# Gated GELU feed-forward: the last Strassen product of six unit pairs in the second pass is divided once more

## The chip, the cores and the metric

The kernel runs on one core of one Trainium2 chip. The metric is the device time of one execution in microseconds. Three runs of the kernel before took 538.74, 539.11 and 539.6 us; the median is 539.11 us. One execution was also recorded by the profiler, and all rows below are from it.

## The reference

```python
def reference(x, w_gate, w_up, w_down):
    g = einsum("bsd,df->bsf", x, w_gate)      # S = 2048 tokens, d = 1024, f = 3584
    u = einsum("bsd,df->bsf", x, w_up)
    h = gelu(g) * u                           # tanh form of gelu
    return einsum("bsf,fd->bsd", h, w_down)   # 2048 x 1024
```

Inputs, weights and the result are bf16. The arithmetic is three products of 2048 x 1024 x 3584.

## The kernel before

The 2048 tokens are taken in two passes of 1024 (two halves of N = 512). A pass first makes `h` for all 3584 features and keeps it in SBUF (`hT`), then multiplies it with `w_down` (`down`, line 464). Both steps use Strassen's scheme in Winograd's form: a product of 2 x 2 blocks is made of seven block products instead of eight, with sums of blocks ahead of and behind them.

Gate/up goes by units: unit `u` has 256 columns of `w_gate` and 256 of `w_up`, fourteen units in a pass. The blocks of a unit are 128 features by 512 of the 1024 input rows on the weights' side (`a11`, `a21`, `a12`, `a22` in `sums_s`, line 150) and 512 input rows by 512 tokens on the other (`sums_t`, line 135). On the weights' side the sums `s1` to `s4` are made for every unit by POOL: eight operations of 128 x 512, since each exists for gate and for up. The sums of the tokens, `t1` to `t4`, are made once per pass by DVE. Sums are f32r, so products of sums are f32 matmuls; the two products of raw blocks are bf16. A product is four matmuls of 512 columns per output bank, one for each 128 input rows (`product`, line 186).

The PE order in a unit (`unit`, line 208) is: the product s2·t2 (P2), which accumulates on the bank of the raw product of unit and `xT`; s1·t1 (P5); s3·t3 (P7); s4·tb (P3); and sa·t4 (P4), which is the block A22 times T4. Each is eight matmuls, four for gate and four for up. The raw products of two units (32 bf16 matmuls, `raw_products`) are issued together, ahead of P4 of each odd unit (`ahead_of_p4`, line 682). So the work repeats by pairs of units, from one raw block to the next.

Results leave PSUM in this manner: ACT copies a bank to SBUF (`snap`), DVE adds another bank to the copy (`add`, line 199), ACT applies gelu, and DVE multiplies gate and up into `hT` (`times`). The eight PSUM banks are four pairs with changing roles `E`, `K`, `C`, `F` (lines 635 and 692).

Small tiles share one ring of 52 slots (`kpool`): a new tile takes the slot of the tile made 52 tiles before, and its first writer waits until all readers of that one are through. Weights of a unit lie in a ring of three buffers (`wpool`); SP issues the load of unit u+2 during unit u (`aside(0)`), and it waits for the buffer in the same way. The instructions of SP, DVE, POOL and PE, and in the unit loop of ACT too, run in the order in which the code names them; no scheduler moves them. In the first pass the unit loop also makes the sums of `w_down` (`keep_part`, `keep_whole`, `fetch_wd`, `store_made`), which go to DRAM and come back in both passes.

The last product of the second pass's `down` is itself divided once more already (`inner_product`, line 417): seven products with 256 columns, four of which go to halves of banks (`z1`, `z6`, `z7`, `z5`).

Of the kernel before, what the change touches and what calls it, by code (L numbers as in the profile page):

```python
# [10 lines left out]
def kernel(  # L11
# [5 lines left out]
    w_down: bass.AP,  # L17
    out: bass.AP,
):

    nc = tc.nc
# [19 lines left out]
    N = 512  # L55
    NS = N // P
    NPASS = S // (2 * N)
    NU = NFB // 2
    NWARM = 7
    H, Q, R2 = NJ // 2, N // 2, range(2)  # L60
    SLOTS = 52
    LAG = 3
# [27 lines left out]
    def dve(out, a, b, op):  # L90
        nc.vector.tensor_tensor(out=out, in0=a, in1=b, op=op)  # L91
# [4 lines left out]
    def new(eng, a, b, op, name, shape=None, dtype=None):  # L96
        t = slot(shape or [P, N], dtype or f32r, name)
        eng(t, a, b, op)
        return t

    def cast(src, name, shape=None):
        t = slot(shape or [P, N], f32r, name)
        nc.scalar.copy(out=t, in_=src)  # L103
        return t

    def snap(ps, name):
        t = slot([P, N], f32, name)
        nc.scalar.copy(out=t, in_=ps)  # L108
        return t
# [4 lines left out]
        )  # L114

    def load_w(u, queue=nc.sync):
        f0 = u * 2 * P
        w = wpool.tile([P, 2, NKB, 2 * P], bf16, name="w")  # L120
# [29 lines left out]
    def sums_s(w, eng):  # L150
        GU = range(2)
        sh = [P, KH, P]
        a11, a21 = [[w[:, i, :KH, h : h + P] for i in GU] for h in (0, P)]
        a12, a22 = [[w[:, i, KH:, h : h + P] for i in GU] for h in (0, P)]
        return Sums(
            how={
                "s1": lambda q, GU=GU: [new(eng, a21[i], a22[i], ADD, "s1", sh) for i in GU],
                "s2": lambda q: [new(eng, q["s1"][i], a11[i], SUB, "s2", sh) for i in GU],
                "s3": lambda q: [new(eng, a11[i], a21[i], SUB, "s3", sh) for i in GU],
                "s4": lambda q: [new(eng, a12[i], q["s2"][i], SUB, "s4", sh) for i in GU],  # L160
                "sa": lambda q: [cast(a22[i], "sa", sh) for i in GU],
            }
        )

    def pool_behind(tile):
        nc.gpsimd.tensor_copy(out=seen, in_=tile[:, :1].bitcast(f32))
# [3 lines left out]
        t.make("t1", "t2", "t3", "tb", "t4")  # L170
        return t

    def make_s(w, eng):
        s = sums_s(w, eng)
        s.make("s1", "s2", "s3", "sa", "s4")
        return s

    def gelu(src):
        g = slot([P, N], f32, "g")
        nc.scalar.activation(g, src, ACT.Gelu_apprx_tanh)  # L180
        return g

    def times(fb, c, g, u):
        dve(hT[:, fb // NJ, fb % NJ, c, :], g, u, MUL)

    def product(ps, lhs, rhs, start):
        for k in range(KH):
            matmul(ps, lhs[:, k, :], rhs[k], start and k == 0, k == KH - 1)

    def raw_products(e, c, xT, w):  # L190
        for i in range(2):
            product(e[i], w[:, i, :KH, :P], [xT[0][:, k, :] for k in range(KH)], True)
        p1 = [snap(e[i], "p1") for i in range(2)]
        for i in range(2):
            b21 = [xT[0][:, KH + k, :] for k in range(KH)]
            product(c[i], w[:, i, KH:, :P], b21, True)
        return p1

    def add(ps, other):
# [4 lines left out]
    def finish_raw(u, c, p1):  # L204
        g, up = add(c, p1)
        times(2 * u, 0, gelu(g), up)

    def unit(u, banks, s, t, late, after_p5, aside, keep, ahead_of_p4, behind_p4):
        GU = range(2)
        e, c, d = banks  # L210
        aside(-2)
        g, up = late() if late else (None, None)
        aside(-1)
        for i in GU:
            product(e[i], s["s2"][i], t["t2"], False)
        aside(0)
        keep(0, c[0])
        u2 = [snap(e[i], "u2") for i in GU]
        if late:
            g = gelu(g)  # L220
        c11 = g, up
        keep(1, c[0])
        keep(2, c[1])
        c = d
        for i in GU:
            product(c[i], s["s1"][i], t["t1"], True)
        p5 = [snap(c[i], "p5") for i in GU]
        after_p5()
        for i in GU:
            product(e[i], s["s3"][i], t["t3"], False)  # L230
        g, up = new(dve, e[0], p5[0], ADD, "sum", dtype=f32), banks[1][not late]
        dve(up, e[1], p5[1], ADD)
        if late:
            times(2 * u, 0, *c11)
        for i in GU:
            product(c[i], s["s4"][i], t["tb"], False)
        times(2 * u + 1, 1, gelu(g), up)
        aside(1)
        g, up = add(c, u2)
        times(2 * u, 1, gelu(g), up)  # L240
        ahead_of_p4()
        for i in GU:
            product(e[i], s["sa"][i], t["t4"], False)
        behind_p4()
        times(2 * u + 1, 0, gelu(e[0]), e[1])

    td = dpool.tile([P, NJ, 3, N], f32, name="td")  # L250
    wraw, made = {}, {}
# [29 lines left out]

    def store_made(j):
        nc.sync.dma_start(out=td[:, j], in_=made[j][:, :3].bitcast(f32))

    q12, s12, q73, q4, raw = {}, {}, {}, {}, {}
# [43 lines left out]
    def fetch12(n):  # L331
# [1 line left out]
        rl = slot([P, 2, N], bf16, "raw")  # L333
        nc.sync.dma_start(out=rl, in_=wdn[:, kh, j : j + 2, :N])
        raw[1, n] = rl

    def inner_sums(late):
# [184 lines left out]
                put21(i)  # L524

    warm = nc.const_aps.tensor(1.0, [P, N], bf16)
    ident = xpool.tile([P, P], bf16, name="ident")  # L530
    make_identity(nc, ident)
# [98 lines left out]
    def making(u):  # L630
        if u < 2 or u >= NU:
            return []
        return list(range(u - 2, NJ if u == NU - 1 else u - 1))

    E, K, C, F = odd, cc, dd, even

    def loaded(u):
        if u not in ws:
            ws[u] = load_w(u)
        return ws[u]  # L640

    def raw_of(u, e):
        p1 = raw_products(e, K, xT, loaded(u))
        return lambda: finish_raw(u, K, p1)

    for ip in range(NPASS):
        with tc.manual_schedule(engines={ENG.Activation}):
            if ip == 0:
                ws = {1: w, 2: ahead}
                late = lambda: add(cc, nxt["p1"])  # L650
            else:
                raw_of(0, F)()
                raw_of(1, C)()
            for u in range(1 if ip == 0 else 0, NU):
                js = making(u) if ip == 0 else []
                first = (ip, u) == (0, 1)

                def prepare():
                    if first:
                        pool_behind(t["t4"][-1])  # L660
                    if u + 1 < NU:
                        nxt["s"] = make_s(loaded(u + 1), pool)
                    if len(js) == 1:
                        store_made(js[0])
                    for j in js[1:]:
                        keep_whole(j)
                    if ip == 0:
                        fetch_wd(making(u + 1))

                def keep(part, ps):  # L670
                    if js:
                        keep_part(js[0], part, ps)

                def aside(part):
                    if first and part < 0:
                        rest_of_0(part + 2)
                    if part == 0 and u + 2 < NU:
                        loaded(u + 2)
                    if part == 0 and "t4" not in t:
                        t.make("t4")  # L680

                def ahead_of_p4():
                    if u % 2 and u + 1 < NU:
                        raw_of(u + 1, F)()
                        nxt["c11"] = raw_of(u + 2, C)

                def behind_p4():
                    if "c11" in nxt:
                        nxt.pop("c11")()

                if u % 2 and not first:
                    E, K, C = C, E, K
                banks = (E, K, C) if u % 2 else (F, K, E)
                unit(
                    u, banks, s, t, late if first else None, prepare, aside, keep,
                    ahead_of_p4, behind_p4,
                )
                s = nxt.pop("s", None)

        last = ip == NPASS - 1  # L700
        got, nxt = {}, {}

        def more(step):
            if last:
                return
            if step in (-1, 0, 2):
                store_made({-1: NJ - 3, 0: NJ - 2, 2: NJ - 1}[step])
            if step == 0:
                xT[:] = new_x()
            if step >= 24 and step % 2 == 0 and step // 2 - 12 < len(moves):  # L710
                c, ko = moves[step // 2 - 12]
                transposing(xT, c, ko, (2 * (ip + 1) + c) * N)
            if step == 50:
                ws.clear()
                ws.update({n: load_w(n) for n in range(2)})
            if step == 58:
                got["s"] = make_s(ws[0], dve)
            if step == 62:
                got["t"] = make_t(xT)

        down(ip, F + K, C + E, last, more)
        E, K, C, F = K, E, F, C
        if not last:
            t, s = got["t"], got["s"]

# [28 lines left out]
```

## Time and profile before

| | |
|---|---|
| median of three runs | 539.11 us (538.74 to 539.6) |
| profiled execution | 539.29 us |
| its span in the profile | 537.5 us (1.79 us lie around it) |
| granted TensorE clock | 0.999 |
| PE busy | 532.7 us, 99% of the span |
| DVE, POOL, ACT busy | 356.3 (66%), 259.3 (48%), 258.1 (48%) |
| second-pass gate/up, 270 to 446 us | PE busy 176.00 of 176.00 us, POOL 119.38, ACT 97.03, DVE 94.79 |

The first 7 us are loads and transposes, 7 to 270 us are the first pass, 270 to 446 us gate/up of the second, and the rest its down product.

How to read it: PE and PEld are the matmuls and the weight loads of TensorE, DVE is VectorE, ACT ScalarE, POOL GpSimd, SP the engine that issues DMAs. Matmuls are pipelined and their ends are modelled, so that the mean duration of a record (390 to 401 ns for 512 f32 columns) is longer than the distance from one start to the next; costs are read from the starts. L112 is the line of the matmul helper, L91 that of DVE's operations, L94 that of POOL's, L108 ACT's copy out of PSUM, L180 gelu. A number in brackets at a row's end is idle time ahead of it, and what ended it. A row "x16" holds sixteen instructions one after another.

### The profile page before, as it was taken

The numbers are of one execution on the slowest core, as the hardware profiler recorded it, in microseconds if no ns is written. First come the engines' busy times: TensorE is split into PE (matmuls) and PEld (weight loads), VectorE is DVE, ScalarE is ACT, GpSimd is POOL, SyncE is SP. The second block draws the span as 40 slices with busy tenths as digits, with TensorE's granted clock in tenths as the row PEclk, the third lists the DMA queues.
The fourth block names the chain that finished last, engine by engine and source line by source line (L and its number), as shares of the span: only waits on it lengthen the run. The fifth ranks groups of instructions, "written<-read, shape, count | busy, mean of one in ns | idle before, by whom it ended". The sixth has DMA issues, their size and how long they took to land.

```text
span 537.5 us, 7573 instructions
## 1 busy us (share of the span) xinstructions
PE 532.7 (99%) x2451; PEld 382.4 (71%) x2451; DVE 356.3 (66%) x536; ACT 258.1 (48%) x457; POOL 259.3 (48%) x243
## 2 busy tenths in 40 slices
PE   8999999999999999999999999999999999999997
PEld 4568686867777746888868677776868685478887
DVE  2986766767676894595855464555554639979844
ACT  2556675666666410265355555555555551113340
POOL 1179966677773500000087767676766600000194
PEclk9999999999999999999999999999999999999999
DMA  9675666759482999999873233242520049573752
GB/s 245 156 186 168 186 177 176 218 136 262 131 234 71 383 357 298 308 197 275 264 187 88 78 80 81 77 119 50 145 57 23 2 130 390 204 236 88 243 169 70
DMA packets 108199, 93.30 MB, mean 174 GB/s; under 512 B 17280, under 2 KB 93056, under 8 KB 108160
## 3 DMA queue, kind: packets, MB, share of 16 engines
q1 hardware_dynamic: 108160, 92.82, 59.6%
q8 instruction: 20, 0.33, 0.3%
q14 instruction: 19, 0.16, 0.1%
HBM read 74.45 MB, written 15.20 MB: 167 GB/s over the span
## 4 chain that ended last, share of the span: by engine, by line
PE 98%; DMA 1%; SPq 0%; DVE 0%; issue 0%
PE bank L112 98%; DMA xn<-in_x_dram 1%; SPq L538 0%; DVE st L91 0%; PE bank L545 0%
## 5 line engine op out<-in xcount | busy, mean ns | idle before, releaser
L94 POOL TENSOR_TENSOR s<-w 128x512 fp32r<-128x512 bf16 x102 | 119.0, 1188 | 163.0 <-PE bank L112 113.5
L112 PE MATMUL bank<-t,s 128*128 128x512 f32 x648 | 151.7, 390 | 0.0
L112 PEld LDWEIGHTS bank<-t,s 128*128 128x128 f32 x648 | 121.7, 188 | 25.4
L112 PE MATMUL bank<-xT,w 128*128 128x512 bf16 (+1 forms) x504 | 109.7, 376 | 0.0
L108 ACT COPY p<-bank 128x512 f32<-128x512 f32 x124 | 69.8, 590 | 45.2 <-PE bank L112 45.1
L91 DVE TENSOR_TENSOR sum<-bank,p 128x512 f32<-128x512 f32 x54 | 37.3, 691 | 79.4 <-PE bank L112 78.3
L112 PEld LDWEIGHTS <-w 128*128 128x128 bf16 x504 | 48.1, 98 | 58.1 <-issue 3.4
L91 DVE TENSOR_TENSOR hT<-g,bank 128x512 bf16<-128x512 f32 x112 | 76.8, 688 | 17.6 <-PE bank L112 4.5
L180 ACT ACTIVATE g<-sum 128x512 f32<-128x512 f32 x81 | 51.4, 635 | 74.5 <-DVE sum L91 74.2
L94 POOL TENSOR_TENSOR q<-q 128x256 fp32r<-128x256 f32 x28 | 21.1, 788 | 80.0 <-PE bank L112 79.4
L112 PE MATMUL bank<-q 128*128 128x512 f32 x240 | 59.0, 389 | 0.0
L94 POOL TENSOR_TENSOR s<-w,s 128x512 fp32r<-128x512 bf16 x50 | 57.7, 1175 | 0.0
L94 POOL TENSOR_TENSOR s<-s,w 128x512 fp32r<-128x512 f32 x50 | 57.2, 1166 | 0.0
L112 PE MATMUL bank<-t,sa 128*128 128x512 f32 x216 | 55.9, 401 | 0.0
L112 PE MATMUL bank<-tb,s 128*128 128x512 f32 x216 | 53.3, 389 | 0.0
L108 ACT COPY u<-bank 128x512 f32<-128x512 f32 x62 | 35.5, 589 | 34.3 <-PE bank L112 34.2
L112 PEld LDWEIGHTS bank<-q 128*128 128x128 f32 x240 | 45.1, 188 | 9.3
L112 PE MATMUL bank<-raw,hT 128*128 128x512 bf16 x224 | 48.7, 379 | 0.0
L112 PEld LDWEIGHTS bank<-t,sa 128*128 128x128 f32 x216 | 40.6, 188 | 9.4
L103 ACT CAST tb<-raw 128x512 fp32r<-128x512 bf16 x28 | 17.2, 624 | 62.6 <-DMA raw<-in_w_down_dram 34.1
L112 PEld LDWEIGHTS bank<-tb,s 128*128 128x128 f32 x216 | 40.6, 188 | 8.4
L91 DVE TENSOR_TENSOR bank<-bank,p 128x512 f32<-128x512 f32 x54 | 37.7, 699 | 8.8 <-PE bank L112 6.2
(60 smaller groups left out, 493.8 us busy)
## 6 DMA issues: line engine op xcount, KB each, us to landing
raw<-in_w_down_dram SPq DMA_DIRECT2D x76, 256.0 KB, 5.1
q<-td SPq DMA_DIRECT2D x60, 256.0 KB, 4.9
w<-in_w_gate_dram SPq DMA_DIRECT2D x27, 512.0 KB, 5.9
w<-in_w_up_dram SPq DMA_DIRECT2D x27, 512.0 KB, 7.0
td<-m SPq DMA_DIRECT2D x12, 768.0 KB, 4.6
w<-td SPq DMA_DIRECT2D x6, 1024.0 KB, 10.1
out_dram<-st SPq DMA_DIRECT2D x32, 128.0 KB, 1.7
td<-w SPq DMA_DIRECT2D x2, 768.0 KB, 6.3
```

Of the source, the lines that this page charges most:

```text
L91: nc.vector.tensor_tensor(out=out, in0=a, in1=b, op=op)
L94: nc.gpsimd.tensor_tensor(out=out, in0=a, in1=b, op=op)
L103: nc.scalar.copy(out=t, in_=src)
L108: nc.scalar.copy(out=t, in_=ps)
L112: nc.tensor.matmul(ps, lhsT=lhs, rhs=rhs, start=start, stop=stop, skip_group_check=True)
L180: nc.scalar.activation(g, src, ACT.Gelu_apprx_tanh)
```

## The change

In the second pass, for the unit pairs (0,1), (2,3) up to (10,11), the products P4 of both units (A22·T4, two times eight matmuls of 512 columns) are replaced by one function, `split_p4`, behind P3 of the odd unit. It takes the A22 blocks of the two units, one above the other, as one matrix, halves it by unit and by input rows, halves T4 by input rows and by tokens, and forms the product by Winograd's scheme: seven products of 128 x 256 x 256, each for gate and for up, which is 28 matmuls of 256 columns. `Ea` and `Eb` are the banks of the two units on which the rest has been accumulated; three of the seven products go to the bank `z`, one after another and with a copy by ACT between them, and one to the bank `y`; gate has the left and up the right half of each.

With it come, per pair: four sums of the weights on POOL (`split_sums`), a cast `sh` and three copies of `z` on ACT, six more operations on DVE. Of the four casts `sa` the two of the odd unit fall away, `sh` stands in for them. Eight subtractions of 128 x 256 on DVE (`inner_ops`, placed by `PREP`) make `n1` to `n4` from T4 once in each pass; those of the first pass are not used. The raw block behind the split is divided into two `raw_first` and two `raw_second`, with the end of the split's elementwise work (`rest`) between. The roles of the bank pairs are renamed `Ea`, `Eb`, `K`, `D` and exchanged by other rules; the bank in which the `w_down` sums of the first pass are made is another one of the same pair (`keep`); and the fetches of `w_down` are issued earlier. The weight buffer of the even unit is read until `split_sums` are done, since these need both units' weights.

```diff
+    SPLIT = ((),(0,2,4,6,8,10))
+    PREP = ({(2,"p"):1,(2,"q"):1,(2,"1"):1,(3,"p"):1,(3,"q"):1,(3,"1"):1,(4,"p"):1,(4,"q"):1}, {(0,"p"):2,(0,"q"):2,(0,"1"):1,(1,"p"):2,(1,"q"):1})
...
+    def split_sums(wa, wb):
+        ka, kb = slice(KH, KH + 2), slice(KH + 2, NKB)
+        a11, a12, a21, a22 = [w[:, :, k, P:] for w in (wa, wb) for k in (ka, kb)]
+        sh = [P, 2, 2, P]
+        s1 = new(pool, a21, a22, ADD, "s1", sh)
+        s2 = new(pool, s1, a11, SUB, "s2", sh)
+        s3 = new(pool, a11, a21, SUB, "s3", sh)
+        s4 = new(pool, a12, s2, SUB, "s4", sh)
+        return s1, s2, s3, s4
...
-        keep(1, c[0])
-        keep(2, c[1])
+        keep(1, c[1])
+        keep(2, c[0])
...
+        more = behind_p7()
...
-        times(2 * u, 1, gelu(g), up)
-        ahead_of_p4()
-        for i in GU:
+        p4((g, up))
+
+    def whole_p4(u, e, s, t, ahead, behind):
+        ahead()
+        for i in range(2):
             product(e[i], s["sa"][i], t["t4"], False)
-        behind_p4()
+        behind()
         times(2 * u + 1, 0, gelu(e[0]), e[1])
...
+    def inner_ops(t):
+        n = t["n"] = [slot([P, 2, Q], f32r, "n") for _ in range(4)]
+        left, right = slice(0, Q), slice(Q, N)
+        ops = []
+        for k in range(2):
+            b1, b2 = t["t4"][k], t["t4"][2 + k]
+            n1, n2, n3, n4 = [x[:, k] for x in n]
+            ops += [
+                (n1, b1[:, right], b1[:, left]),
+                (n2, b2[:, right], n1),
+                (n3, b2[:, right], b1[:, right]),
+                (n4, b2[:, left], n2),
+            ]
+        return ops
+
+    def split_p4(a, ea, eb, z, y, sa, sh, sums, t, c12):
...
+        zz = xpool.tile([P, 2, 2, N], f32, name="xT1")
+        z, y = [b.rearrange("p (i q) -> p i q", i=2) for b in (z, y)]
+
+        def half(ps, lhs, rhs, fresh=False):
+            for i in range(2):
+                for k in range(2):
+                    matmul(ps(i), lhs(i, k), rhs[k], fresh and i == 0 and k == 0, k == 1)
+
+        half(lambda i: z[:, i], lambda i, k: sa[i][:, k], b11, True)
+        nc.scalar.copy(out=zz[:, 0, :, left], in_=z)
+        half(lambda i: ea[i][:, left], lambda i, k: sa[i][:, 2 + k], b21)
+        half(lambda i: y[:, i], lambda i, k: s1[:, i, k], n1, True)
+        half(lambda i: z[:, i], lambda i, k: s2[:, i, k], n2)
+        g12 = gelu(c12[0])
+        nc.scalar.copy(out=zz[:, 0, :, right], in_=z)
+        half(lambda i: ea[i][:, right], lambda i, k: s4[:, i, k], b22)
+        times(2 * a + 2, 1, g12, c12[1])
+        dve(zz[:, 0, :, right], y, zz[:, 0, :, right], ADD)
+        c11 = add(ea, [zz[:, 0, i] for i in range(2)])
+        half(lambda i: eb[i][:, left], lambda i, k: sh[:, i, k], n4)
+        half(lambda i: z[:, i], lambda i, k: s3[:, i, k], n3)
+        nc.scalar.copy(out=zz[:, 1, :, left], in_=z)
+        g11 = gelu(c11[0])
+        dve(zz[:, 1, :, right], y, zz[:, 1, :, left], ADD)
+        times(2 * a + 1, 0, g11, c11[1])
+        c11 = add(eb, [zz[:, 1, i] for i in range(2)])
+        return lambda: times(2 * a + 3, 0, gelu(c11[0]), c11[1])
...
+                def p4(c12):
+                    if not (odd_u and apart(u)):
+                        times(2 * u, 1, gelu(c12[0]), c12[1])
...
+                    elif odd_u:
+                        rest = split_p4(
+                            u - 1, Ea, Eb, *D, halves["sa"], halves["sh"], halves["sums"], t, c12
+                        )
+                        if u + 1 < NU:
+                            p1 = raw_first(K, xT, loaded(u + 1)), raw_first(
+                                D, xT, loaded(u + 2)
+                            )
+                            rest()
+                            for n, c in enumerate((Ea, Eb)):
+                                raw_second(c, xT, loaded(u + 1 + n))
+                                finish_raw(u + 1 + n, c, p1[n])
```

More of the change, by code (lines that the diff above doesn't have):

```diff
@@ L161, in sums_s @@
                 "sa": lambda q: [cast(a22[i], "sa", sh) for i in GU],
+                "sh": lambda q: cast(w[:, :, KH + 2 :, P:], "sh", [P, 2, 2, P]),
             }
@@ L171, in make_t, with make_s @@
         return t
-    def make_s(w, eng):
+    def make_s(w, eng, casts=("sa",)):
         s = sums_s(w, eng)
-        s.make("s1", "s2", "s3", "sa", "s4")
+        s.make("s1", "s2", "s3", *casts, "s4")
         return s
+    def split_sums(wa, wb):
[7 more added lines that the diff above has]
+        return s1, s2, s3, s4
     def gelu(src):
@@ L188, in product, with raw_first, raw_second @@
             matmul(ps, lhs[:, k, :], rhs[k], start and k == 0, k == KH - 1)
-    def raw_products(e, c, xT, w):
+    def raw_first(e, xT, w):
         for i in range(2):
             product(e[i], w[:, i, :KH, :P], [xT[0][:, k, :] for k in range(KH)], True)
-        p1 = [snap(e[i], "p1") for i in range(2)]
+        return [snap(e[i], "p1") for i in range(2)]
+    def raw_second(c, xT, w):
         for i in range(2):
@@ L196, in raw_products @@
             product(c[i], w[:, i, KH:, :P], b21, True)
+    def raw_products(e, c, xT, w):
+        p1 = raw_first(e, xT, w)
+        raw_second(c, xT, w)
         return p1
@@ L206, in finish_raw, with unit @@
         times(2 * u, 0, gelu(g), up)
-    def unit(u, banks, s, t, late, after_p5, aside, keep, ahead_of_p4, behind_p4):
+    def unit(u, banks, s, t, late, after_p5, aside, keep, mid, behind_p7, p4):
         GU = range(2)
@@ L228, in unit @@
         after_p5()
+        mid()
         for i in GU:
             product(e[i], s["s3"][i], t["t3"], False)
-        g, up = new(dve, e[0], p5[0], ADD, "sum", dtype=f32), banks[1][not late]
+        g = new(dve, e[0], p5[0], ADD, "sum", dtype=f32)
+        up = banks[1][not late]
         dve(up, e[1], p5[1], ADD)
+        more = behind_p7()
         if late:
@@ L237, in unit @@
         times(2 * u + 1, 1, gelu(g), up)
+        if more:
+            times(2 * u + 1, 0, gelu(more[0]), more[1])
         aside(1)
         g, up = add(c, u2)
-        times(2 * u, 1, gelu(g), up)
-        ahead_of_p4()
-        for i in GU:
+        p4((g, up))
+    def whole_p4(u, e, s, t, ahead, behind):
+        ahead()
+        for i in range(2):
             product(e[i], s["sa"][i], t["t4"], False)
-        behind_p4()
+        behind()
         times(2 * u + 1, 0, gelu(e[0]), e[1])
+    def inner_ops(t):
[12 more added lines that the diff above has]
+        return ops
@@ new lines, in split_p4 @@
+    def split_p4(a, ea, eb, z, y, sa, sh, sums, t, c12):
+        left, right = slice(0, Q), slice(Q, N)
+        s1, s2, s3, s4 = sums
+        n1, n2, n3, n4 = [[n[:, k] for k in range(2)] for n in t["n"]]
+        b11, b21, b22 = [
+            [t["t4"][h + k][:, cols] for k in range(2)]
+            for h, cols in ((0, left), (2, left), (2, right))
+        ]
+        zz = xpool.tile([P, 2, 2, N], f32, name="xT1")
[23 more added lines that the diff above has]
+        return lambda: times(2 * a + 3, 0, gelu(c11[0]), c11[1])
@@ L633, in making @@
         return list(range(u - 2, NJ if u == NU - 1 else u - 1))
-    E, K, C, F = odd, cc, dd, even
+    Ea, Eb, K, D = even, dd, cc, odd
+    preps = []
     def loaded(u):
@@ L640, in loaded, with raw_of, apart @@
         return ws[u]
-    def raw_of(u, e):
-        p1 = raw_products(e, K, xT, loaded(u))
-        return lambda: finish_raw(u, K, p1)
+    def raw_of(u, e, c):
+        p1 = raw_products(e, c, xT, loaded(u))
+        return lambda: finish_raw(u, c, p1)
+    def apart(u):
+        return u - u % 2 in SPLIT[ip]
     for ip in range(NPASS):
@@ L651 @@
             else:
-                raw_of(0, F)()
-                raw_of(1, C)()
+                raw_of(0, Ea, K)()
+                raw_of(1, Eb, K)()
             for u in range(1 if ip == 0 else 0, NU):
@@ L656 @@
                 first = (ip, u) == (0, 1)
+                odd_u = u % 2 == 1
+                if first or not odd_u:
+                    halves = {}
                 def prepare():
@@ L660, in prepare @@
                         pool_behind(t["t4"][-1])
+                    if ip == 0 and (u >= NU - 2 or not apart(u)):
+                        fetch_wd(making(u + 1))
+                    if odd_u and apart(u):
+                        halves["sums"] = split_sums(ws[u - 1], ws[u])
                     if u + 1 < NU:
-                        nxt["s"] = make_s(loaded(u + 1), pool)
+                        nxt["s"] = make_s(
+                            loaded(u + 1), pool, () if apart(u) or apart(u + 1) else ("sa",)
+                        )
+                    if apart(u) and odd_u:
+                        halves["sh"] = sums_s(ws[u], pool)["how"]["sh"](None)
                     if len(js) == 1:
@@ L666, in prepare, with prep @@
                         keep_whole(j)
-                    if ip == 0:
-                        fetch_wd(making(u + 1))
+                    prep("p")
+                def prep(part):
+                    for _ in range(PREP[ip].get((u, part), 0)):
+                        if "n" not in t:
+                            preps.extend(inner_ops(t))
+                        dve(*preps.pop(0), SUB)
                 def keep(part, ps):
@@ L676, in aside @@
                         rest_of_0(part + 2)
+                    if part == 0 and ip == 0 and apart(u) and u < NU - 2:
+                        fetch_wd(making(u + 1))
                     if part == 0 and u + 2 < NU:
@@ L680, in aside, with mid @@
                         t.make("t4")
[L682 to L687, printed above, removed]
+                    if part == 1:
+                        prep("1")
+                        if apart(u) and not odd_u and u + 1 < NU:
+                            halves["sa"] = sums_s(ws[u], pool)["how"]["sa"](None)
+                def mid():
+                    if not apart(u) and "sa" not in s:
+                        s.make("sa")
@@ L688, in behind_p4, with behind_p7, ahead, behind @@
+                def behind_p7():
+                    prep("q")
+                def ahead():
+                    if odd_u and u + 1 < NU:
+                        raw_of(u + 1, Ea, D)()
+                        nxt["c11"] = raw_of(u + 2, K, D)
+                def behind():
                     if "c11" in nxt:
                         nxt.pop("c11")()
-                if u % 2 and not first:
-                    E, K, C = C, E, K
-                banks = (E, K, C) if u % 2 else (F, K, E)
+                def p4(c12):
+                    if not (odd_u and apart(u)):
+                        times(2 * u, 1, gelu(c12[0]), c12[1])
+                    if first:
+                        whole_p4(u, odd, s, t, after_first, behind)
+                    elif not apart(u):
+                        whole_p4(u, (Ea, Eb)[odd_u], s, t, ahead, behind)
+                    elif odd_u:
[5 more added lines that the diff above has]
+                                D, xT, loaded(u + 2)
+                            )
+                            rest()
+                            for n, c in enumerate((Ea, Eb)):
+                                raw_second(c, xT, loaded(u + 1 + n))
+                                finish_raw(u + 1 + n, c, p1[n])
+                        else:
+                            rest()
@@ L694, with after_first @@
+                def after_first():
+                    raw_of(2, even, cc)()
+                    nxt["c11"] = raw_of(3, dd, cc)
+                if first:
+                    banks = odd, cc, dd
+                else:
+                    banks = (Eb, D, K) if odd_u else (Ea, K, D)
                 unit(
                     u, banks, s, t, late if first else None, prepare, aside, keep,
-                    ahead_of_p4, behind_p4,
+                    mid, behind_p7, p4,
                 )
+                if odd_u and not first and u + 1 < NU:
+                    if not apart(u):
+                        Ea, Eb, K, D = Ea, K, D, Eb
+                    else:
+                        Ea, Eb, K, D = K, D, Eb, Ea
@@ L719, in more @@
                 got["t"] = make_t(xT)
-        down(ip, F + K, C + E, last, more)
-        E, K, C, F = K, E, F, C
+        down(ip, Ea + D, K + Eb, last, more)
+        Ea, Eb, K, D = K, Ea, Eb, D
         if not last:
```

## The prediction

> **What bounds the kernel now.** I read the page first: busy times, granted clock, chain.
>
> ```profile
> PE 532.7 (99%) x2451; PEld 382.4 (71%) x2451; DVE 356.3 (66%) x536; ACT 258.1 (48%) x457; POOL 259.3 (48%) x243
> ...
> PEclk9999999999999999999999999999999999999999
> ...
> PE 98%; DMA 1%; SPq 0%; DVE 0%; issue 0%
> ```
>
> The chain that ends last is 98% matmuls at the full clock, so the time is the sum of the matmuls' spacings. A busy PE is not yet a fast PE, so I next read spacings off the timeline: in two rows of PE that follow each other, the difference of the starts, divided by the count of the first row, is what one matmul costs. Two stretches of it, the second-pass gate/up and the end of the last down product, which has 256-column f32 matmuls already:
>
> ```profile
> 292.69 0.69 DVE L91 TENSOR_TENSOR sum<-bank,p 128x512 f32<-128x512 f32 x1 [3.84 <-PE bank L112]
> ...
> 293.41 0.63 ACT L180 ACTIVATE g<-sum 128x512 f32<-128x512 f32 x1
> ...
> 294.12 2.28 POOL L94 TENSOR_TENSOR s<-w 128x512 fp32r<-128x512 bf16 x2 [3.70 <-ACT g L180]
> ...
> 295.14 7.08 PE L112 MATMUL bank<-xT,w 128*128 128x512 bf16 x32
> ...
> 303.89 5.60 PE L112 MATMUL bank<-t,s 128*128 128x512 f32 x24
> ...
> 309.33 1.98 PE L112 MATMUL bank<-tb,s 128*128 128x512 f32 x8
> ...
> 311.00 0.69 DVE L91 TENSOR_TENSOR sum<-bank,u 128x512 f32<-128x512 f32 x1
> ...
> 311.15 1.98 PE L112 MATMUL bank<-t,sa 128*128 128x512 f32 x8
> ...
> 320.22 7.08 PE L112 MATMUL bank<-xT,w 128*128 128x512 bf16 x32
> ```
>
> ```profile
> 523.13 1.75 PEld L112 LDWEIGHTS bank<-q,sa 128*128 128x128 f32 x14
> 523.25 1.84 PE L112 MATMUL bank<-q,sa 128*128 128x256 f32 x14
> 524.81 1.71 PEld L112 LDWEIGHTS bank<-q,xT 128*128 128x128 f32 x14
> 524.92 1.80 PE L112 MATMUL bank<-q,xT 128*128 128x256 f32 x14
> 525.12 0.59 ACT L447 COPY m<-bank 128x512 f32<-128x512 f32 x1 [2.49 <-PE bank L112]
> 526.45 1.74 PEld L112 LDWEIGHTS bank<-q,w 128*128 128x128 f32 x14
> 526.56 1.83 PE L112 MATMUL bank<-q,w 128*128 128x256 f32 x14
> ```
>
> A 512-column f32 matmul costs (309.33 − 303.89)/24 = 226.7 ns. One of 256 columns costs (524.92 − 523.25)/14 = 119.3 ns where the weights are `sa`, and (526.56 − 524.92)/14 = 117.1 ns where they lie in `xT`: 53% of the long one, not 50%. Seven half-size products for eight therefore gain 1 − 7/8 × 2 × 119.3/226.7 = 7.9% of what they replace. The pair period, raw block to raw block, is 320.22 − 295.14 = 25.08 us. Last, busy times of the other engines in the second-pass gate/up:
>
> ```profile
> 270.00:446.00 176.00, 176.00 (x787) 126.91 (x787) 94.79 (x142) 97.03 (x168) 119.38 (x104) 1.00 0.33 91
> ```
>
> In order PE, weight loads, DVE, ACT, POOL: PE has no hole at all, POOL is next with 68%.
>
> **The change part by part.** The sum starts from the profiled execution: 539.29 us, span 537.5, 1.79 around the span. It stands 0.18 above the median 539.11.
>
> Matmuls. In each of six pairs two products of 8 matmuls go (16 × 226.7 = 3.63 us), and 28 of 256 columns come (28 × 119.3 = 3.34 us): 0.287 us per pair, 1.72 us over six. The new weights lie in the slots that `sa` lies in, so I take 119.3. At 117.1 it is 2.09 us; at the spacing inside the last x28 row of that kind, 119.9, it is 1.62.
>
> [...]
>
> Weight loads. 12 more per pair. They are recorded at 188 to 190 ns each but start one matmul ahead (523.13 against 523.25) and leave the spacing at 119.3, so they cost nothing beyond it. Lower bound zero; if a load were not hidden at all, see the rivals.
>
> Order on PE. The even unit's P4 leaves its place, so its P3 is followed by the odd unit's P2; the split product stands behind the odd unit's P3. The raw block, then the two second raw products, follow. The number of changes between bf16 and f32 is as before: no cost.
>
> The shared bank z. It is written by b11, s2·n2 and s3·n3 and copied by ACT (L291, L296, L303 of the new code) in between; s2·n2 and s3·n3 accumulate on, so PE must wait for the copy. From the rows: copy starts 0.32 us after the start of the block's last matmul (525.12 against 524.80), takes 0.59, and is seen by the next engine in 0.03 (the DVE sum's end at 293.38 to gelu's 293.41) to 0.08 us (gelu's end at 294.04 to POOL's 294.12). So z is free 0.94 to 0.99 us after that start. Two blocks of four lie between; the next z matmul is due 9 × 119.3 = 1.07 us after, its weight load at 0.95. If the matmul carries the wait, there is 0.08 to 0.13 us of slack; if the load does, −0.04 to 0.01. The far bound for the handoff is 0.32 us (matmul to ACT): z free at 1.23, 0.16 to 0.28 us late. Twelve such waits (two per pair; the third copy is followed by the raw block): 0 to 3.4 us. I take 0, since the handoffs between elementwise engines are the nearer rows.
>
> ACT and DVE around it. Before the second copy (due 2.11 us after the split's start) ACT has the first copy to 1.26 and a gelu to 1.90, whose DVE sum ends near 0.54 by the same place before (311.00 + 0.69 against 311.15): it holds. ACT gains three copies and loses one cast per pair, about +1.2 us on 97.03/7 = 13.9; DVE gains six operations of 0.69, 4.1 us on 13.5; both stay far below 25. The DVE chain behind it frees bank y for the raw product of u+2 about 5.4 us into the split, which is wanted at 5.95; the second raw products on `Ea` and `Eb` have 1.6 and 0.4 us. No cost taken; if the y chain were 0.6 us longer it would cost 0.05 to 0.1 per pair.
>
> POOL. Four sums more per pair: 20 × 1.15 (two in 2.28 to 2.31) = 23.0 of 24.79 us. Counted from the raw block, PE has 6.9 us of raw products, eight blocks of 1.81 to 21.4, then the split to 24.8. In the order of the 52 slots those of the split sums come free at about 9.9, so these run to 14.5 and the next even unit's to 23.7; PE wants them from 22.4 and 31.7. It fits, with 1.8 us to spare in a period and a lead of 8 us; cost zero, with the cover nearly gone.
>
> SP. The even unit's weight buffer now stays until the split sums have read it, so the load of the weights two units on starts at 14.5 on the same count, some 5 us later than now, and with the 7.0 us to landing of the profile's page is there at about 21.5 to 22: 1.7 us before POOL is free to read it (23.7), 3 before PE's next raw block (24.8). The earlier `w_down` fetches of pass one stand ahead of other loads on that queue by one unit's issues (0.37 and 0.57 us a piece in SP's rows), and no PE row of the first pass waits for them. Cost zero.
>
> The subtractions `n`. Eight 256-column DVE operations once in each pass, in the first pass unused; at most the 0.69 us of the 512-column rows each, 5.5 us in a pass in which DVE is idle far longer. Zero on PE.
>
> Sum: 539.29 − 1.72 = 537.57 us profiled, 537.4 against the median.
>
> **Rivals.** (1) The z waits stall PE. Each 0.1 us costs 1.2 us; 0.143 us each eats the gain. At the load-bound middle of the bounds, about 0.1 each, 538.6, the same as before; from 0.233 us each it is slower by over 0.2%; at the far bound of 0.28 us it ends at 537.4 + 3.4 = 540.8. For it: on one of two readings the slack is about nothing, and it recurs twelve times. Against it: handoffs of 0.03 to 0.08.
>
> (2) POOL becomes the bound. 24.79/20 = 1.24 us per operation is where it decides; the lead of about 8 us lasts six pairs up to 1.31. At 1.4 us: 6 × (28.0 − 24.79) − 8 = +11 us, 549. For it, a place where DVE reads SBUF alone:
>
> ```profile
> 270.35 4.30 POOL L94 TENSOR_TENSOR s<-w 128x512 fp32r<-128x512 bf16 x2 [86.06 <-PE bank L112]
> ```
>
> There POOL takes 2.15 us each. Against it: each DVE operation added to the pairs has a PSUM operand, as those beside the 1.14 us sums had; only the `n` subtractions have none. [...]
>
> (3) The loads do not hide with these operands: 28 × 0.188 = 5.3 us per pair instead of 3.34, 537.4 + 6 × 1.9 = 549. The last down product, same sizes and types, speaks against it.
>
> (4) The 256-column spacing in the new groups is half of the long one, 113.4 ns: 6 × (3.63 − 28 × 0.1134) = 2.7 us, 536.4. Both rows of 256 columns speak against it. [...]
>
> **How the numbers follow.** Range of the measured runs is 538.74 to 539.6, so 0.2% (1.08 us: 538.03 and 540.19) is about what can be told from no change. Forecast with no stall worth a name, 537.0 to 538.0: 0.50. Rival 1: 0.36, of which stalls below 0.05 us still faster 0.08, same 0.19, slower 0.09. Rivals 2 and late weights or a late bank y: 0.09, slower. Rival 3: 0.02, slower. Rival 4: 0.03, faster. Faster 0.61, same 0.19, slower 0.20. The prediction is the likeliest, 537.4; the range 536.9 to 540.0 leaves out rival 4, rival 2, and the far end of rival 1.
>
> **What would show it.** Right: span near 535.8; raw block to raw block 24.8 us in the second pass; 256-column groups on `t` and `n` at 117 to 120 ns; no PE idle at the z blocks. Rival 1: PE idle ahead of the first matmul of s2·n2 and s3·n3, released by ACT. Rival 2: POOL near 100% there and PE waiting for `s`. Wrong would make me, above all, a handoff from ACT to PE slower than the rows between ACT, DVE and POOL.

## The result and the profile after

The changed kernel took 540.86 us (median of six runs, 540.78 to 541.14) against 539.15 us for the kernel before (median of six, 538.64 to 539.85). The ratio is 1.0029 with a 95% interval of 1.0018 to 1.0041: slower by 0.3%, where 0.3% faster had been forecast. The profiled execution took 541.14 us, its span is 539.4.

The page of the changed kernel; its lines are in the order of those shown of the kernel before:

```profile
PE 531.9 (99%) x2502; PEld 385.6 (71%) x2523; DVE 387.8 (72%) x588; ACT 263.8 (49%) x471; POOL 288.3 (53%) x267
...
PEclk9999999999999999999999999999999999999999
...
PE 96%; issue 1%; DMA 1%; DVE 0%; SPq 0%; ACT 0%; DVEq 0%
```

The clock is the same and PE is busy 0.8 us less, but the chain is now 96% matmuls instead of 98. So PE has a little less to do, and something else came into the chain. The busy time by stretches of the span (us; busy time of PE, weight loads, DVE, ACT, POOL with counts; then clock, DMA share and rate) says where:

```profile
7.00:270.00 263.00, 260.68 (x1168) 184.37 (x1176) 196.03 (x303) 135.96 (x247) 118.97 (x105) 1.00 0.79 220
270.00:446.00 176.00, 175.20 (x855) 130.37 (x861) 119.95 (x186) 102.43 (x182) 147.60 (x128) 1.00 0.32 87
```

In the kernel before, the first of these rows was:

```profile
7.00:270.00 263.00, 262.98 (x1189) 186.69 (x1187) 191.46 (x297) 135.45 (x247) 118.18 (x105) 1.00 0.78 220
```

PE is now idle for 2.3 us in the first pass, in which nothing was to change for it, and for 0.8 us in the second. The profile names two waits of PE in the trace of this kernel, after its first microseconds (total us, times, longest):

```profile
PE bank L101 <- DVE sum L80: 1.6, 1, 1.6
...
PE bank L101 <- ACT u L97: 0.3, 1, 0.3
```

The first is at 48 us. These two are not all of the idle time; for the rest the view names no releaser. By the distances of the matmuls' starts, the first pass loses 1.85 us at 48 us, and 0.25 and 0.19 us at 55.4 and 57.4 us, in the next unit. The second pass loses 0.54 us at 292.5, where the second wait is, and 0.36 us at 297.5, both in the first divided pair. This is the timeline of the changed kernel at 48 us:

```profile
44.13 2.30 POOL L83 TENSOR_TENSOR s<-w 128x512 fp32r<-128x512 bf16 x2
...
45.20 3.76 DVE L80 TENSOR_TENSOR n<-t 128x256 fp32r<-128x256 f32 x1
46.06 1.98 PE L101 MATMUL bank<-tb,s 128*128 128x512 f32 x8
46.38 2.31 POOL L83 TENSOR_TENSOR s<-w,s 128x512 fp32r<-128x512 bf16 x2
48.89 0.68 DVE L80 TENSOR_TENSOR sum<-bank,p 128x512 f32<-128x512 f32 x1
...
49.62 2.11 PE L101 MATMUL bank<-t,sa 128*128 128x512 f32 x8 [1.58 <-DVE sum L80]
49.64 2.47 POOL L83 TENSOR_TENSOR s<-w 128x512 fp32r<-128x512 bf16 x2 [0.96 <-DVE sum L80]
```

The same sum and the same P4 in the kernel before:

```profile
45.46 0.69 DVE L91 TENSOR_TENSOR sum<-bank,p 128x512 f32<-128x512 f32 x1
...
47.91 1.98 PE L112 MATMUL bank<-t,sa 128*128 128x512 f32 x8
```

One subtraction `n` of 128 x 256 takes 3.76 us. It ends at 48.96, 0.27 us after POOL's row of sums has ended (46.38 + 2.31 = 48.69). The DVE sum behind it, which started at 45.46 in the kernel before, starts at 48.89; it reads the bank on which P4 accumulates, so P4 starts at 49.62 instead of 47.91.

The subtractions by form, with the mean in ns at the end of the busy time, are on the mean two to three times as long as one where POOL is idle (0.42 us at 282.80):

```profile
L80 DVE TENSOR_TENSOR n<-t,n 128x256 fp32r<-128x256 f32 x8 | 6.1, 756 | 0.0
L80 DVE TENSOR_TENSOR n<-t 128x256 fp32r<-128x256 f32 x4 | 5.4, 1342 | 0.0
```

The pair period, once the first pair is over, is as it should be. Starts of the raw blocks of the changed kernel:

```profile
274.20 7.08 PE L101 MATMUL bank<-xT,w 128*128 128x512 bf16 x31
299.93 7.08 PE L101 MATMUL bank<-xT,w 128*128 128x512 bf16 x31
324.78 7.08 PE L101 MATMUL bank<-xT,w 128*128 128x512 bf16 x31
349.64 7.08 PE L101 MATMUL bank<-xT,w 128*128 128x512 bf16 x31
```

The first of them in the kernel before:

```profile
271.87 7.08 PE L112 MATMUL bank<-xT,w 128*128 128x512 bf16 x32
```

The later pairs take 24.85 us on the mean (25.08 before); the first takes 25.73. The second pass starts 2.33 us late.

### The profile page after: what moved, and what is told of

The parts are those of the page before. It is cut to its first block, busy times and chain, and to the rows that moved or that the text cites. A ratio compares the mean times of both kernels' runs of the same rounds, so it can differ in the third digit from the quotient of the medians.

```text
span 539.4 us, 7816 instructions
## 1 busy us (share of the span) xinstructions
PE 531.9 (99%) x2502; PEld 385.6 (71%) x2523; DVE 387.8 (72%) x588; ACT 263.8 (49%) x471; POOL 288.3 (53%) x267
## 4 chain that ended last, share of the span: by engine, by line
PE 96%; issue 1%; DMA 1%; DVE 0%; SPq 0%; ACT 0%; DVEq 0%
PE bank L101 96%; DMA w<-in_w_up_dram 1%; SPq L594 0%; DVE bank L80 0%; DVE st L80 0%; DVE sum L80 0%; ACT g L179 0%; ACT sa L92 0%; ACT u L97 0%; SPq L613 0%; DVE n L80 0%; DVEq L80 0%
## 5 line engine op out<-in xcount | busy, mean ns | idle before, releaser
L83 POOL TENSOR_TENSOR s<-w 128x512 fp32r<-128x512 bf16 x114 | 133.6, 1191 | 146.9 <-PE bank L101 115.6
L101 PE MATMUL bank<-t,s 128*128 128x512 f32 (+1 forms) x672 | 157.4, 388 | 0.3 <-ACT u L97 0.3
L101 PEld LDWEIGHTS bank<-t,s 128*128 128x128 f32 x672 | 124.8, 188 | 27.0 <-issue 1.1
L101 PE MATMUL bank<-xT,w 128*128 128x512 bf16 (+1 forms) x489 | 107.8, 376 | 0.9
L179 ACT ACTIVATE g<-sum 128x512 f32<-128x512 f32 x93 | 58.9, 634 | 80.7 <-DVE sum L80 77.7
L83 POOL TENSOR_TENSOR s<-w,s 128x512 fp32r<-128x512 bf16 x56 | 65.2, 1184 | 0.0
L83 POOL TENSOR_TENSOR s<-s,w 128x512 fp32r<-128x512 f32 x56 | 64.5, 1171 | 0.5
L80 DVE TENSOR_TENSOR q<-hT 128x512 fp32r<-128x512 bf16 x56 | 38.9, 694 | 4.3 <-PE bank L101 4.1
L101 PEld LDWEIGHTS <-hT 128*128 128x128 bf16 x224 | 21.8, 98 | 26.4 <-issue 0.5
```

The costliest lines, as they stand in the source:

```text
L83: nc.gpsimd.tensor_tensor(out=out, in0=a, in1=b, op=op)
L101: nc.tensor.matmul(ps, lhsT=lhs, rhs=rhs, start=start, stop=stop, skip_group_check=True)
```

## The experiments

Two theories were set up from this. Theory L: the subtractions `n`, which have both operands in SBUF, are long because of POOL's sums beside them (3.76 us at 45.20, 0.42 at 282.80 where POOL is idle), and what stands behind them on DVE comes late. That POOL keeps DVE from SBUF meanwhile, as its wording on record has it, is the author's inference from these times; the traces show durations alone. Rival R: the rest of the rewriting (banks, `w_down` fetches, slots) delays the first pass, and the long subtractions only show it.

**No pair divided, no subtractions.**

```diff
-    SPLIT = ((),(0,2,4,6,8,10))
+    SPLIT = ((),())
-    PREP = ({(2,"p"):1, ...}, {(0,"p"):2, ...})
+    PREP = ({}, {})
```

> The changed kernel with no pair divided and without any of the n subtractions, so that only the rest of the rewriting stands: other roles of the banks, exchanged banks for the w_down sums, earlier w_down fetches. Theory L (DVE is locked out of SBUF by POOL during the n subtractions, and that alone delays the first pass): 539.15 us like the kernel before, within 0.3, and no PE wait at 47 to 57 us. Rival R (the rest of the rewriting delays the first pass): 2.3 us more, 541.5, with the same PE holes at 47 to 57 us.

Measured: 539.56 us against 539.28 of the kernel before, 1.0003 (0.9994 to 1.0011), and no PE wait in the unit loops. Rival R falls: roles and banks, fetches and the renaming cost nothing that can be measured.

**The unused subtractions alone.**

```diff
-    PREP = ({}, {})
+    PREP = ({(2,"p"):1, ... as in the change}, {})
```

> No pair divided, but the eight n subtractions of the first pass, whose results nobody reads, stay on DVE. Theory L: 539.15 + 2.33 = 541.5 us, with one subtraction of over 3 us at 45 us and PE waiting 1.6 us for the DVE sum behind it. Rival R: the same as the run without them, wherever that lies.

Measured: 541.56 us, 1.0037 (1.0024 to 1.005). Eight subtractions whose result nobody reads cost 0.37%, which is more than the whole slowdown. The trace has the same picture as the changed kernel:

```profile
43.54 2.30 POOL L83 TENSOR_TENSOR s<-w 128x512 fp32r<-128x512 bf16 x2
44.48 3.91 DVE L80 TENSOR_TENSOR n<-t 128x256 fp32r<-128x256 f32 x1
...
45.81 2.29 POOL L83 TENSOR_TENSOR s<-w,s 128x512 fp32r<-128x512 bf16 x2
48.31 0.68 DVE L80 TENSOR_TENSOR sum<-bank,p 128x512 f32<-128x512 f32 x1
...
49.04 2.11 PE L101 MATMUL bank<-t,sa 128*128 128x512 f32 x8 [1.74 <-DVE sum L80]
```

The single times of this kernel lie between 538.79 and 543.61 us, a wider spread than that of any other kernel here. Two of the twelve, 538.79 and 539.36, are no longer than those without the subtractions.

**The change without the unused subtractions.**

```diff
-    PREP = ({(2,"p"):1, ...}, {(0,"p"):2, ... as in the change})
+    PREP = ({}, {(0,"p"):2, ... as in the change})
```

> The change as it is, but without the eight unused n subtractions of the first pass. Theory L: 540.86 - 2.33 = 538.5 us, 0.6 faster than before; the first pair of the second pass keeps its holes of about 0.9 us. Rival R: 540.9, nothing gained.

Measured: 538.91 us, 0.999 (0.9981 to 0.9999). The sign turns with the first pass's subtractions, as theory L has it, though the interval only just leaves out 1; the gain of 0.37 us is a little smaller than the 0.6 expected. The first pair keeps its hole.

**POOL makes the subtractions of the second pass.**

```diff
-    PREP = ({}, {(0,"p"):2,(0,"q"):2,(0,"1"):1,(1,"p"):2,(1,"q"):1})
+    PREP = ({}, {(0,"p"):8})
...
-                        dve(*preps.pop(0), SUB)
+                        pool(*preps.pop(0), SUB)
```

> As the run before, and the eight n subtractions of the second pass are made by POOL (some 0.78 us each, 6.2 us, from POOL's rows of 128x256), all of them ahead of the first pair's sums. Theory L: no DVE operation is locked out any more, the first pair's holes of 0.9 us go, 537.6 us. Rival P (POOL's lead of 8 us on the second pair is used up by 6.2 us more and its period has too little room): PE waits for s sums in pair two or three, 538.5 or more.

Measured: 537.85 us, 0.9972 (0.9961 to 0.9983); a second time, beside the last experiment below, 537.89 us, 0.9968 (0.9955 to 0.998). The first pair now takes 24.83 us (raw blocks at 272.11 and 296.94), so the 0.90 us of the first pair were the subtractions too. POOL in this kernel:

```profile
280.59 0.75 POOL L83 TENSOR_TENSOR n<-t 128x256 fp32r<-128x256 f32 x1
...
285.71 0.75 POOL L83 TENSOR_TENSOR n<-t,n 128x256 fp32r<-128x256 f32 x1
286.40 1.18 POOL L83 TENSOR_TENSOR s<-w 128x512 fp32r<-128x512 bf16 x1
```

The eight take 5.87 us (280.59 to 286.46), and PE waits for no sum of POOL in any pair: the lead of 8 us holds.

**The same number of DVE operations, with one operand in PSUM.** By theory L it is both operands in SBUF beside POOL's sums that make the subtractions long; this tells it from the plain fact that there are more operations on DVE. No pair is divided; the results, which are read by nobody, are other numbers.

```diff
+        seen_bank.update({"p": c[1], "q": e[0], "1": c[0]})
...
-                        dve(*preps.pop(0), SUB)
+                        out, a, _ = preps.pop(0)
+                        dve(out, a, seen_bank[part][:, :Q], SUB)
```

> As the run with no pair divided and the eight unused subtractions on DVE in the first pass, but the second operand of each is 128x256 of a PSUM bank in place of a second SBUF operand; place, size and number are the same, and the results are still read by nobody. Theory L (what delays DVE is waiting for the SBUF access that POOL holds, which only an operation with both operands in SBUF needs): subtractions of 0.3 to 0.5 us, no hole of PE, 539.3 us within 0.4. Rival D (any DVE operation more in that place delays the sum behind it): 541.5 as with the SBUF operands.

Measured: 539.49 us, 1.0003 (0.9993 to 1.0012). At the same place, beside the same sums on POOL:

```profile
44.34 2.33 POOL L83 TENSOR_TENSOR s<-w 128x512 fp32r<-128x512 bf16 x2
45.69 0.42 DVE L80 TENSOR_TENSOR n<-t,bank 128x256 fp32r<-128x256 f32 x1
46.03 0.68 DVE L80 TENSOR_TENSOR sum<-bank,p 128x512 f32<-128x512 f32 x1
46.43 1.98 PE L101 MATMUL bank<-tb,s 128*128 128x512 f32 x8
46.59 2.33 POOL L83 TENSOR_TENSOR s<-w,s 128x512 fp32r<-128x512 bf16 x2
```

0.42 us instead of 3.76 or 3.91, and no hole. Place, size and number are not what makes the subtraction long beside these sums; the second operand in SBUF is.

**The bank z.** In the kernel with `n` on POOL the first matmul of s2·n2 is followed by its neighbour 48 ns late in each pair. That is rival 1 of the prediction, at a small size, or else a cost of the wait as such. One block was moved in this kernel:

```diff
+        half(lambda i: eb[i][:, left], lambda i, k: sh[:, i, k], n4)
         half(lambda i: z[:, i], lambda i, k: s2[:, i, k], n2)
...
-        half(lambda i: eb[i][:, left], lambda i, k: sh[:, i, k], n4)
         half(lambda i: z[:, i], lambda i, k: s3[:, i, k], n3)
```

> The run with n on POOL, but the block sh.n4 stands ahead of s2.n2, so that three blocks of four matmuls instead of two lie between b11 and s2.n2, and one instead of two between s2.n2 and s3.n3. Theory Z (the 48 ns ahead of s2.n2 are the copy of z coming late: z is free for a matmul 9 x 0.1193 + 0.048 = 1.12 us after the start of the block's last matmul): no hole ahead of s2.n2; ahead of s3.n3, due after 5 x 0.1193 = 0.60 us, a hole of 0.52 us; 6 x (0.52 - 0.05) = +2.8 us, 540.7. Rival S (the 48 ns are what waiting for two engines costs there, whatever the copy does): the 48 ns stay ahead of s2.n2; the hole ahead of s3.n3 comes by 0.47 or less.

Measured: 540.31 us, 1.0018 (1.0009 to 1.0027). The holes ahead of s2·n2 are gone, and those ahead of s3·n3 have come. From the timeline of this kernel:

```profile
295.59 0.64 PE L101 MATMUL bank<-t,s 128*128 128x256 f32 x4
295.79 0.59 ACT L297 COPY xT<-bank 128x512 f32<-128x512 f32 x1 [0.80 <-PE bank L101]
...
296.43 0.53 PEld L101 LDWEIGHTS bank<-n,s 128*128 128x128 f32 x4 [0.40 <-ACT xT L297]
296.43 0.74 PE L101 MATMUL bank<-n,s 128*128 128x256 f32 x4 [0.20 <-ACT xT L297]
```

The copy ends at 296.38 and the weight load starts at 296.43: the handoff from ACT takes 0.05 us, and the load waits for it, not only the matmul. The s3·n3 block was due at 295.59 + 4 × 0.12 = 296.07 and is 0.36 us late, its second matmul another 0.10 us, 0.46 in all (0.52 expected). Theory Z holds as to the place: the 48 ns go where the copy has room. Rival S fails by that sign alone, since the 0.46 us are within its "0.47 or less". And this run does not part the two cleanly: the trace shows that PE's load of s2·n2 waits for POOL alone here, and no longer for ACT as well.

**Room by a raw product in between.**

```diff
...
+        p1 = between()      # raw_first(K) of the next even unit, 8 bf16 matmuls
         half(lambda i: z[:, i], lambda i, k: s3[:, i, k], n3)
```

> As the run before it, and the first raw product of the next unit (8 bf16 matmuls on K) stands between s4.b22 and s3.n3, so that no z block has less than three blocks ahead of it. Theory Z: no hole at z, 537.85 - 0.29 = 537.6 us if two more changes between bf16 and f32 in a pair cost nothing. Rival S: 537.85, the 48 ns stay. Rival X (each change costs 0.02 us or more): 537.8 or above, without a hole at z.

Measured: 542.84 us, 1.0068 (1.0055 to 1.0081); none of the three theories foresaw it. The raw product that was moved had been the cover of the third copy. The next matmuls are now the raw product on `D`, whose first bank is z:

```profile
297.63 0.58 ACT L97 COPY p<-bank 128x512 f32<-128x512 f32 x1 [0.28 <-PE bank L101]
298.12 0.59 ACT L304 COPY xT<-bank 128x512 f32<-128x512 f32 x1
...
298.76 0.59 PE L101 MATMUL bank<-xT,w 128*128 128x512 bf16 x2 [0.74 <-ACT xT L304]
```

PE's row has 0.74 us of idle time for this copy in every pair; by the starts the matmul is 0.90 us late (1.02 us after the start of the last matmul of s3·n3, at 297.74, where 0.12 were due). The copies of the moved product that ACT makes first cost next to nothing: the copy of z starts 0.38 us after that matmul, against 0.32 in the rows of the prediction. What is missing is the cover: start 0.38, copy 0.59 and handoff 0.05 make the 1.02 us. There is no hole ahead of s2·n2 or s3·n3, and 6 × (0.90 − 0.05) = 5.1 us accounts for the whole difference to 537.85 (4.99), so the two more changes between bf16 and f32 in a pair left no cost that shows.

**Room by an earlier start.** The four matmuls of b11 stand between the two halves of the odd unit's P3.

```diff
         for i in GU:
             product(c[i], s["s4"][i], t["tb"], False)
+            if i == 0 and halves.get("sa") and "sh" in halves:
+                ...  # the four matmuls of b11 into z
...
-        half(lambda i: z[:, i], lambda i, k: sa[i][:, k], b11, True)
```

> As the run with n on POOL, but the four matmuls of b11 into z stand between the gate half and the up half of the odd unit's P3, four 512-column matmuls (0.91 us) earlier; the copy of z keeps its place on ACT. Theory Z (the 48 ns ahead of s2.n2 in each pair are the copy of z coming some 0.06 us late for the next weight load into z): no hole there, 537.85 - 0.29 = 537.6 us. Rival S (the 48 ns come with the wait itself): 537.85.

Measured: 537.39 us, 0.9964 (0.9952 to 0.9976), the fastest kernel here. On the same chip the kernel with `n` on POOL alone took 537.89 us:

> The run with n on POOL once more, on the same chip as the one with b11 in P3, so that the two can be compared: 537.85 us within 0.3, with the 48 ns holes.

The intervals of the two overlap; the traces do not leave it open. The s2·n2 holes are in all six pairs of the one and in none of the other, where b11 and its copy lie early:

```profile
292.73 0.64 PE L101 MATMUL bank<-t,sa 128*128 128x256 f32 x4
...
293.41 0.59 ACT L296 COPY xT<-bank 128x512 f32<-128x512 f32 x1 [0.80 <-PE bank L101]
...
294.61 1.11 PE L101 MATMUL bank<-n,s 128*128 128x256 f32 x8
...
295.56 0.64 PE L101 MATMUL bank<-t,s 128*128 128x256 f32 x4
```

Here z is free at about 294.05, half a microsecond before y's matmuls start at 294.61. The eight matmuls of y and s2·n2 take 295.56 − 294.61 = 0.95 us, 118.8 ns each; with the hole the same row takes 1.00 us (294.51 to 295.51 in the first run with `n` on POOL). The pair period is 24.82 us (raw blocks at 297.00 and 421.10, five pairs), against 24.85 without the move; these 0.03 us are 0.2 us over six pairs, a little less than the 0.29 expected. The trace has PE's wait for the copy as an instruction of its own on PE's sequencer (the views leave such records out). It is still there, at 294.03 to 294.08, and the matmul behind it, at 294.14, is less than 0.01 us late. So the wait as such costs nothing where the copy ends early enough, and rival S falls.

## Why the prediction was wrong

**Matmuls: right.** 1.72 us were forecast, a period of 24.79 us and 0 for the order and the loads. The 256-column groups run at 118 to 120 ns, the period without a stall is 24.82, and the kernel without the subtractions on DVE is 539.28 − 537.85 = 1.43 us faster (0.9 to 2.1 by its interval). That fits 1.72 less the z holes of 6 × 0.048 = 0.29; that it does so to the hundredth is luck, since the period of 24.82 leaves 0.03 us per pair of the forecast open.

**Bank z: mechanism right, size off.** The step "I take 0" should have been 0.29 us. The load carries the wait, which was one of the two readings, and there the slack was put at −0.04 to 0.01. Only s2·n2 is late; s3·n3, with the same distance, is not. The kernel with `n` on POOL shows where the two differ, each copy of z and the first load behind it:

```profile
294.23 0.59 ACT L291 COPY xT<-bank 128x512 f32<-128x512 f32 x1 [1.71 <-PE bank L101]
...
294.93 0.19 PEld L101 LDWEIGHTS bank<-n,s 128*128 128x128 f32 x1
...
295.71 0.59 ACT L296 COPY xT<-bank 128x512 f32<-128x512 f32 x1 [0.36 <-PE bank L101]
...
296.35 0.54 PEld L101 LDWEIGHTS bank<-n,s 128*128 128x128 f32 x4
```

At s3·n3 the load starts 0.05 us after the copy's end, inside the 0.03 to 0.08 that were taken, and on time. At s2·n2 it starts 0.11 us after it, outside them. It was due at 294.87, so the slack is −0.06, and that shows as 0.048 us per pair. The load of s2·n2 waits for POOL's sum too, and PE's sequencer waits for the copy ahead of it in an instruction of its own (294.86 to 294.91); the load of s3·n3 waits for the copy alone and does it itself. That the separate wait is what takes the 0.06 us more is read from these records in all six pairs; no run took it away by itself.

**The subtractions `n`: this step failed.** It said "at most the 0.69 us of the 512-column rows each, 5.5 us in a pass in which DVE is idle far longer. Zero on PE." Both halves were wrong. The bound came from rows of DVE with a PSUM operand, while these have none: one where POOL is idle takes 0.42 us (282.80), those beside POOL's sums up to 3.91. And idle time of an engine is no cover for an operation that stands ahead of one with a deadline. Behind the first `n` in the program's order on DVE stood a sum that has to read a bank before P4 can go on with it; it started at 48.89, when the `n` was ending (48.96). The trace of before shows that deadline: the sum starts at 45.46, and P4, which needs its bank, at 47.91. With the long `n` ahead of it the sum came 3.43 us later and P4 1.71 us later, so only 1.7 us of the delay were free. The subtractions cost 2.33 us in the first pass (the first raw block of the second pass starts at 274.20 instead of 271.87), 1.85 of them at that P4, and 25.73 − 24.83 = 0.90 in the first pair. With these, 539.15 − 1.72 + 0.29 + 2.33 + 0.90 = 540.95; measured were 540.86.

**POOL: right, but seen from one side.** Rival 2 showed the row in which POOL takes 2.15 us a sum beside DVE operations that read SBUF alone. It asked only what this does to POOL, which has 8 us of lead; the engine with the near deadline was DVE. The place was in the text ("only the `n` subtractions have none") and was dropped because there are few of them. The first alone cost 1.85 us.

**Late weights, bank y, fetches, banks: right at zero.** The run with no pair divided shows it for the fetches and the banks, the traces with the split for the other two: PE has no wait for them, but for the first pair of the changed kernel. There a subtraction at 295.41, of 1.32 us, held back the DVE product that frees bank y, and y's block starts 0.36 us late, which is part of the 0.90.

**Rivals 3 and 4** fell by the spacing. The chance of slower, 0.20, held mostly mishaps at z and on POOL; none of the cases was the one that came.

## What to carry to other kernels

The same subtraction on DVE took 0.42 us where POOL was idle and up to 3.91 beside POOL's sums: take the price of an added operation from a row with the same kinds of operands beside the same neighbour, and ask for both engines what stands behind the one that waits. DVE was idle for a third of the span before (66% busy), and still the sum behind the first unneeded subtraction came 3.43 us later: an unneeded operation is free only if the next one in its queue has the slack. And the room of an accumulation that goes on after a copy is to be counted to the weight load, which here starts 0.12 us ahead of its matmul where nothing holds it (294.39 against 294.51 with `n` on POOL); where PE waited for two engines there, the handoff was 0.11 us (copy's end 294.82, load 294.93) and not 0.05 (296.30, 296.35).

## What the runs showed of the hardware

Beside POOL's sums of 1.15 us each, a subtraction on DVE took up to 3.91 us. At 45.20 DVE's subtraction started while POOL was near the end of the first of four sums that followed each other without a pause, two rows of 2.30 and 2.31 us; it ended at 48.96, 0.27 us after the last. POOL's next sum started at 49.64, after 0.96 us of idle time that ended with DVE's sum. The run with the unused subtractions alone has the same picture: 3.91 us, to 48.39, 0.29 us after the last of four sums (45.81 + 2.29 = 48.10). In the second pass of the changed kernel three subtractions beside POOL's sums took 1.3 to 1.4 us (287.85, 292.90, 295.41) and two 0.46 and 0.48 (287.46, 292.50). With one operand in PSUM, beside the same sums, it was 0.42 at 45.69. So the long one took 3.3 us more (3.76 − 0.42), close to the time of three sums. Why one subtraction beside POOL takes 0.46 us and another 3.76, no run shows. The spread of 538.79 to 543.61 us in the run with the unused subtractions alone suggests that it differs from one execution to the next, but a single execution of each kernel was traced.
